# Attention scores by two halves of TensorE's rows, with another opening

## The chip, the cores and the metric

The kernel runs on one core of one Trainium2 chip. The metric is the device time of one execution in microseconds (us). The core's engines have their own instruction streams: TensorE (PE in the rows; PEld are its weight loads), VectorE (DVE), ScalarE (ACT), GpSimd (POOL) and SyncE (SP), which issues the transfers.

## The reference, cut to what matters

```python
# attention: q, k, v are (8, 8, 576, 64); the keys and values are averaged over 8 neighbours
k_p = k.reshape(B, H, Sp, 8, D).mean(axis=3)      # Sp = 72
v_p = v.reshape(B, H, Sp, 8, D).mean(axis=3)
scores = scale * np.matmul(q, k_p.transpose(0, 1, 3, 2))
attn = np.exp(scores - scores.max(axis=-1, keepdims=True))
attn = attn / (attn.sum(axis=-1, keepdims=True) + 1e-09)
x = np.matmul(attn, v_p)                           # as 4608 tokens x 512
h = x @ w_in                                       # 512 -> 2048
g = np.where(h > 0, h, np.exp(np.minimum(h, 0)) - 1)
x = g @ w_out                                      # 2048 -> 512
h = x @ moe2_w_in                                  # 512 -> 1024
solu = h * softmax(h)
out = layernorm(solu) * g_ln @ moe2_w_out          # 1024 -> 512
```

## The kernel before

**Attention in units.** A unit `i` is one batch and one pair of heads: 32 units, `NP` = 4 to a batch. Its queries lie as `q` [128, 576], the first head's 64 channels on rows 0 to 63, the second's on rows 64 to 127. The summed keys lie for units 4 to 31 in one of two tiles `kpbd` [128, 144] that are zero but for two blocks, head 0 in rows 0 to 63 and columns 0 to 71, head 1 in rows 64 to 127 and columns 72 to 143. So one product of a query tile (128 queries are the weights, 144 columns stream) gives both heads' scores. `att_scores` makes five such products for a unit (`QT` has five query tiles), three into one PSUM bank and two into another (tile `at`, line 517). Each is plain float32, and the trace shows it as two weight loads and two passes. `att_max`, `att_exp` and `att_soft` make the softmax out of PSUM; a unit in `GROUPED` has one ACT instruction for each 72 columns, which also sums them, the others subtract on DVE and have one ACT instruction for all. `att_T` or `att_D` transposes the weights of attention, and `att_V` or `att_VB` multiplies with the values: there the heads go to two halves of TensorE's columns (64 output rows each; lines 670 and 623).

**The rest of TensorE's work** is 512 columns wide in float32r, each product in three parts (high by high, low by high, high by low): `m_h1` and `m_o1` (lines 1052, 1107) for the first three blocks of 512 tokens, `mul_h` and `mul_o` (lines 1247, 1337) for the other six, then the second layer (lines 1444, 1581). Attention of later units is spread between them.

**The order.** Up to the last stage the program is written in a rough order, and `settle` plans the order anew on every engine: it has a cost for each instruction (`cost`), walks through time (`forward`) and writes its order down as dependencies. Neighbouring instructions of TensorE on the same tile are one `Step`, which is not broken up. `startup` writes the opening: units 0 to 3 (`kz`, `kq` tiles), the first weights' conversion from float64, the first products. There are 56 products `busy` on the identity there (line 1658) that keep TensorE at work; the planner puts them into its gaps.

```python
for t0, t1 in ((0, 2), (2, 4)) if i < NP else ((0, 3), (3, 5)):
    s = next(banks)
```

Of the kernel before, what the change touches and what calls it, by code (L numbers as in the profile page):

```python
# [31 lines left out]
def settle(tc, nc, stacks, PEND=2.3, FAST=1.7, FLIGHT=2.5e6, WINDOW=14):  # L32
# [33 lines left out]
    def cost(op, i, ins, outs):  # L66
        n = cols(outs[0])
        if op.eng == "PE":
            if str(ins[0].dtype).endswith("float32r"):
                op.dur += 0.015 + n * 0.0004203  # L70
            elif i.is_transpose:
                op.dur += 0.1045
            else:
                op.dur += 0.226 if n == 144 else 0.04 + n * (0.00084 if outs[0].ap[0][1] == 64 else 0.00168)
            return
        n = max(cols(o) for o in ins + outs)
        wide = [o for o in ins if str(o.bass_ap.tensor.space) == "SB"]
# [20 lines left out]
    for i in list(nc.cur_bb.bb.instructions):  # L98
        kind = type(i).__name__
        if "ManualSchedule" in kind:  # L100
            fixed = len(ops)
        if "ManualSchedule" in kind or "Boundary" in kind:
            continue
        eng = str(i.engine).split(".")[-1]
        if kind == "InstRegisterMove":
            held.setdefault(eng, []).append(i)
            continue
        ins, outs = ([o for o in x if hasattr(o, "bass_ap")] for x in (i.ins, i.outs))
        fi, fo = [foot(o) for o in ins], [foot(o) for o in outs]
        key = fo[0][0] if fo else None  # L110
        if not (eng == "PE" and ops and ops[-1].eng == "PE" and ops[-1].key == key and len(ops[-1].ins) < 12) or idle(key):
            ops.append(Step(eng, len(ops), key))
        op = ops[-1]
        op.ins += held.pop(eng, []) + [i]
        op.acc += [(f, False) for f in fi if not f[0].startswith("in_")] + [(f, True) for f in fo]
        if outs:
            cost(op, i, ins, outs)
# [98 lines left out]
    latest = {}  # L216
# [10 lines left out]
    def forward(latest, until=1e9):  # L227
# [11 lines left out]
        for _ in range(len(ops)):  # L239
            best = min(((x, None, o, x) for o, x in ready[None].items()), key=lambda x: x[0], default=None)  # L240
            for e in engines if best is None else ():
# [2 lines left out]
                    continue  # L244
                if e == "SP" and len(flight) > 7:
                    f = max(f, done[flight[-8]])
                room, behind = FLIGHT, None
                for d in reversed(flight if e == "SP" and f < 40.0 and not manual[e] else ()):
                    room -= d.bytes * d.wide
                    if room < 0.0:  # L250
# [24 lines left out]
                        continue  # L275
                else:
                    first = min(at(o) for o in r)
                    k = min((o for o in r if at(o) <= first + LOOK), key=lambda o: latest[o] + 6.0 * (at(o) - first))
                    for q in r if e in ("Activation", "DVE") else ():
                        end = at(k) + k.dur  # L280
                        if q is not k and at(q) < end:
# [19 lines left out]
            if e is None:  # L301
                done[k] = begin
            elif e == "SP":
                land = PEND if begin > 40.0 else FAST
                for w in range(k.wide):
                    pipe[w] = max(free[e] + land - 1.0, pipe[w]) + k.move * (1.0 if begin > 40.0 else 0.78 if k.wide == 16 else 1.05)
                done[k] = max(pipe[:k.wide]) + 1.0
                flight.append(k)
            else:
                done[k] = free[e] + k.lat  # L310
# [28 lines left out]
def kernel(  # L339
# [49 lines left out]
    zd = [dr.tile([4, P, 256], F32, name=f"zd{i}") for i in range(4)]  # L389
    ident = cst.tile([P, P], F32, name="ident")  # L390
    make_identity(nc, ident)
    kpbd = [pa.tile([P, 2 * SK], F32, name=f"kpbd{i}", tag=f"kpbd{i}", bufs=1) for i in range(2)]
    for t in kpbd:
        nc.gpsimd.memset(t, 0.0)

    def wtile(name):
        return sb.tile([P, 4, 512], F32R, name=name, tag="w", bufs=8)
# [8 lines left out]
    units = [(b, p) for b in range(NB) for p in range(NP)]  # L406
    NU = len(units)

    GROUPED = (1, 2) + tuple(range(4, 22))
    BLOCKT = range(8, 32)  # L410
    NTREE = 3
    KPOOL = ()
    NPOOL = ()

    xh, xl = {}, {}
# [12 lines left out]
    def att_load(i, what="kqv"):  # L428
        b, p = units[i]
        if i < NP:  # L430
            if ("kq", p) not in st:
# [2 lines left out]
                    st["v2"] = p1.tile([P, 4, 512], F32, name=f"v2{i}", tag="wo", bufs=4).rearrange("p a f -> p (a f)")  # L434
                n = P * POOL
                v_t = st["v2"][0:SK, (p % 2) * n:(p % 2 + 1) * n].rearrange("s (c t) -> s c t", t=POOL)
                st["kq", p] = (kq[:, 0:S], kq[:, S:2 * S], v_t)
            k_t, q_t, v_t = st["kq", p]
# [21 lines left out]
    def att_kv(i):  # L460
        b, p = units[i]
        if ("kp", b, p) not in st:
            if i < NP:
                if "kz" not in st:
                    kz = sb.tile([P, 4, 512], F32, name="kz", tag="w", bufs=8)
                    nc.gpsimd.memset(kz[:, :, 0:2 * SK], 0.0)
                    st["kz"] = kz
                kp = st["kz"][:, p, 0:2 * SK]
                vt = st["kz"][0:SK, p, 2 * SK:2 * SK + P]
            else:  # L470
                kp = kpbd[i % 2]
# [12 lines left out]
    def att_kc(i):  # L484
        kp, kr = att_kv(i)[0], st.pop(("kr", i))
        if i in KPOOL:
            nc.gpsimd.tensor_scalar(kp[0:64, 0:SK], kr[0:64, :], 1.0 / (8 * POOL), None, op0=ALU.mult)
            nc.gpsimd.tensor_scalar(kp[64:128, SK:2 * SK], kr[64:128, :], 1.0 / (8 * POOL), None, op0=ALU.mult)
            return
        nc.scalar.mul(kp[0:64, 0:SK], kr[0:64, :], 1.0 / (8 * POOL))  # L490
        nc.scalar.mul(kp[64:128, SK:2 * SK], kr[64:128, :], 1.0 / (8 * POOL))
# [16 lines left out]
    def att_scores(i, banks):  # L508
# [1 line left out]
        kp, vt = st["kp", units[i][0], units[i][1]]  # L510
        q_t = st.pop(("q", i))
        st["sv", i] = []
        for t0, t1 in ((0, 2), (2, 4)) if i < NP else ((0, 3), (3, 5)):
            s = next(banks)
            ts = QT[t0:t1]
            for t, o in enumerate(ts):
# [6 lines left out]
        st["a", i] = (pa.tile([P, NG, SK], F32, name=f"es{i}", tag="es", bufs=2), vt)  # L523

    def grouped(i):
        return i in GROUPED
# [41 lines left out]
    def att_T(i, h):  # L568
# [4 lines left out]
        a = st["aT", i]  # L573
        pt = ps.tile([P, 512], F32, name=f"pt{i}_{h}", tag="C")
        for t in range(4):
            nc.tensor.transpose(pt[0:SK, t * P:(t + 1) * P], es[:, 2 * t + h, :], ident)
        nc.scalar.copy(a[:, h, 0:4 * P], pt[0:SK, :])
        if h == 1 and i >= NP:
            pr = ps.tile([P, 512], F32, name=f"pr{i}", tag="C")
            for g in range(2):  # L580
                nc.tensor.transpose(pr[0:SK, g * P:(g + 1) * P], es[:, 8 + g, :], ident)
# [31 lines left out]

    def att_VB(i, banks):
        es, vt = st.pop(("a", i))
        a = st.pop(("aT", i)).rearrange("k h t -> k (h t)").rearrange("k (r t h c) -> k h r t c", r=4, h=2, c=32)
        b, p = units[i]
        vals = []
        for r, n in ((0, 4), (2, 5)):
# [438 lines left out]
    def m_h1(j, f):  # L1058
        n = sizes[j]
        h = m_mul(j, f, 0, KDM) if (j, f) not in begun else begun.pop((j, f))  # L1060
        e = p1.tile([P, 512], F32, name="e", tag="e")
        nc.scalar.activation(e[:, 0:n], h[:, 0:n], AF.Relu, scale=-1.0)
        nc.scalar.activation(e[:, 0:n], e[:, 0:n], AF.Exp, scale=-1.0)
        gt[j, f] = (e, h)

    def m_max(j, f):
# [733 lines left out]
        i = ((512 * (j + 1) - 1) // S) * NP + NP - 1  # L1800
        return min(NSTEP, 4 * i + (VLAG + 1 if i in BLOCKT else 7))

    goal = [upto(1) + 0, 70, upto(4) + 1]
    def combo_all():
        for k in range(NFP):
            yield from combo_in(k)
# [411 lines left out]
```

## Time and profile before

| | |
|---|---|
| time, median of 3 | 1208.61 us (1208.07 to 1208.61) |
| profiled execution | 1209.54 us, span 1207.8 us |
| PE busy | 1198.3 us (99%) |
| DVE, ACT, POOL busy | 972.2, 835.3, 165.0 us |
| granted TensorE clock | 1.0 |

The span goes from the first to the last instruction of the profiled execution, and 1.7 us of its time lie around it. A matmul's end in the rows is modelled: neighbours overlap, so what a product costs is read from start to start.

### The profile page before, as it was taken

How to read it: one execution, taken by the hardware profiler on the slowest of the kernel's cores; microseconds unless marked ns; L12 is line 12 of the kernel's file. 1: busy time of each engine (PE TensorE's matmuls, PEld its weight loads, DVE VectorE, ACT ScalarE, POOL GpSimd, SP SyncE). 2: the span in 40 equal slices, each digit the busy share in tenths (PEclk: the TensorE clock that was granted, in tenths of full speed). 3: DMA queues.
4: the chain of work that ended last, by engine and by line, in shares of the span. 5: the costliest groups of instructions: out<-in, count | busy, mean ns of one | idle time of the engine just before them, and what ended most of it. 6: DMA issues, size and time to landing. Idle time of an engine off the chain costs nothing.

```text
span 1207.8 us, 17321 instructions
## 1 busy us (share of the span) xinstructions
PE 1198.3 (99%) x5576; PEld 974.4 (81%) x5576; DVE 972.2 (80%) x1509; ACT 835.3 (69%) x1675; POOL 165.0 (14%) x149
## 2 busy tenths in 40 slices
PE   8999999999999999999999999999999999999998
PEld 7877877777887787888888888888888888888887
DVE  6887877788998899977896687996888878778773
ACT  6999877787667773657854488653777766767664
POOL 3455333223211001000000000000000100000000
PEclk9999999999999999999999999999999999999999
DMA  9877689899699998999777988789455444544342
GB/s 317 281 226 222 194 283 288 285 277 317 208 327 279 308 281 282 295 315 271 221 230 240 299 263 298 232 286 346 155 167 168 163 143 153 167 155 143 113 148 96
DMA packets 188875, 285.01 MB, mean 236 GB/s; under 512 B 20208, under 2 KB 99568, under 8 KB 187760
## 3 DMA queue, kind: packets, MB, share of 16 engines
q1 hardware_dynamic: 188784, 283.90, 73.7%
q8 instruction: 44, 0.72, 0.3%
q14 instruction: 47, 0.39, 0.1%
HBM read 191.83 MB, written 92.01 MB: 235 GB/s over the span
## 4 chain that ended last, share of the span: by engine, by line
PE 94%; DVE 2%; POOL 1%; ACT 1%; DMA 1%; issue 1%; SPq 0%; DVEq 0%; ACTq 0%; POOLq 0%
PE hA L1247 16%; PE po L1581 16%; PE oA L1337 13%; PE h L1052 10%; PE o L1107 9%; PE zX L1444 8%; PE zZ L1444 4%; PE oC L1337 4%; PE hB L1247 3%; PE at L517 3%; PE oB L1337 3%; PE at L623 2%; PE zY L1444 2%; PE at L670 1%; DMA w1d<-ci 1%
## 5 line engine op out<-in xcount | busy, mean ns | idle before, releaser
L1581 PE MATMUL po<-w,dhl 128*128 128x512 f32 x864 | 201.3, 389 | 0.0
L1581 PEld LDWEIGHTS po<-w,dhl 128*128 128x128 f32 x864 | 162.1, 188 | 33.6
L1337 PE MATMUL oA<-op,wr 128*128 128x512 f32 x672 | 156.2, 391 | 0.0
L1337 PEld LDWEIGHTS oA<-op,wr 128*128 128x128 f32 x672 | 125.5, 188 | 29.0 <-issue 2.0
L1327 ACT CAST op<-g 128x1024 fp32r<-128x1024 f32 x84 | 87.8, 1053 | 69.3 <-PE oA L1337 30.3
L1328 DVE TENSOR_TENSOR op<-g,op 128x1024 fp32r<-128x1024 f32 x84 | 102.0, 1224 | 17.6 <-ACT op L1327 17.2
L1247 PE MATMUL hA<-sS,wr 128*128 128x512 f32 x414 | 103.3, 391 | 0.0
L1521 POOL TENSOR_TENSOR sc<-sc,mhalf 128x1 f32<-128x1 f32 x36 | 21.4, 597 | 577.8 <-DVE sc L1520 555.7
L1444 PE MATMUL zX<-w,xh 128*128 128x512 f32 x288 | 100.1, 389 | 0.0
L1247 PEld LDWEIGHTS hA<-sS,wr 128*128 128x128 f32 x414 | 77.2, 188 | 17.7 <-ACT sp L1259 0.9
L973 POOL TENSOR_TENSOR wol<-wo,woh 128x512 fp32r<-128x512 f32 x48 | 67.5, 1407 | 149.5 <-ACT woh L972 149.5
L566 POOL TENSOR_TENSOR es<-es,sm 128x720 f32<-128x720 f32 x28 | 43.1, 1541 | 270.5 <-DVE sm L564 227.3
L1107 PE MATMUL o<-gh,woh 128*128 128x512 f32 x192 | 78.2, 407 | 0.0
L1052 PE MATMUL h<-xh,wh 128*128 128x512 f32 x192 | 77.2, 402 | 0.1
L1052 PE MATMUL h<-xh,wl 128*128 128x512 f32 x192 | 75.1, 391 | 0.6 <-POOL wl L869 0.6
L1107 PE MATMUL o<-gh,wol 128*128 128x512 f32 x192 | 75.2, 392 | 0.1
L1052 PE MATMUL h<-xl,wh 128*128 128x512 f32 x192 | 74.9, 390 | 0.0
L1259 ACT COPY sp<-hA 128x512 f32<-128x512 f32 x72 | 42.0, 587 | 36.6 <-PE hA L1247 35.9
L550 ACT ACTIVATE es<-at,mx 128x72 f32<-128x72 f32 x196 | 60.1, 332 | 4.4 <-DVE mx L536 3.7
L1444 PEld LDWEIGHTS zX<-w,xh 128*128 128x128 f32 x288 | 54.1, 188 | 11.2
L1454 ACT COPY sn<-zX 128x512 f32<-128x512 f32 x54 | 31.8, 588 | 43.2 <-PE zX L1444 43.1
L1267 DVE SCALAR_TENSOR_TENSOR g<-ep,g 128x512 f32<-128x512 f32 x72 | 50.1, 699 | 14.0 <-ACT ep L1266 13.7
(387 smaller groups left out, 2800.1 us busy)
## 6 DMA issues: line engine op xcount, KB each, us to landing
wr<-w3d SPq DMA_DIRECT2D x168, 256.0 KB
wr<-w1d SPq DMA_DIRECT2D x161, 256.0 KB
dT<-zd SPq DMA_DIRECT2D x132, 128.0 KB
raw<-in_w SPq DMA_DIRECT2D x32, 512.0 KB
v<-in_v SPq DMA_DIRECT2D x32, 288.0 KB
x1r<-x1d SPq DMA_DIRECT2D x9, 1024.0 KB
out<-ot SPq DMA_DIRECT2D x35, 256.0 KB
zd<-ha SPq DMA_DIRECT2D x17, 512.0 KB
```

The source lines that it names most:

```text
L550: nc.scalar.activation(es[:, g, :], sv[:, g - g0, :], AF.Exp, bias=mx[:, g:g + 1], accum_out=st["sm", i][:, g:g + 1])
L566: eng.tensor_tensor(es, es, bc(sm, n), op=ALU.mult)
L973: nc.gpsimd.tensor_tensor(ol, t[:, f % 4, :], oh.bitcast(F32), op=ALU.subtract)
L1052: nc.tensor.matmul(h[:, 0:n], a[g][:, kk, fo:fo + P], x[j][:, kk, 0:n], start=(kk == 0 and m == 0), stop=(kk == KDM - 1 and m == 2), skip_ ...
L1107: nc.tensor.matmul(acc, a[:, dm * P:(dm + 1) * P], x[:, 0:n], start=(f == 0 and m == 0), stop=(f == NF - 1 and m == 2))
L1247: nc.tensor.matmul(bank, w[:, a, kk], x[:, b, kk], start=(start and m == 0), stop=(stop and m == 5), skip_group_check=True,)
L1267: gate["dve"] = nc.vector.scalar_tensor_tensor(d, e, 1.0, h, op0=ALU.subtract, op1=ALU.max).ins
L1327: gate["act"] = nc.scalar.copy(o[:, 0], src).ins
L1328: gate["dve"] = nc.vector.tensor_tensor(o[:, 1], src, o[:, 0].bitcast(F32), op=ALU.subtract).ins
L1337: nc.tensor.matmul(banks[d], ws[i][:, a, d * P:(d + 1) * P], o[:, b, i], start=(start and t == 0 and i == 0 and m == 0), stop=(stop and t ...
L1444: nc.tensor.matmul(bank, x[:, o:o + P], w[:, y + k, :], start=(start and m == 0), stop=(stop and m == 5), skip_group_check=True,)
L1581: nc.tensor.matmul(po, a[:, c], b[c // 4][:, c % 4, :], start=(m == 0), stop=(m == 3 * NC2 - 1))
```

## The change

Units 4 to 31: the keys of both heads stay in the same 72 columns (`kph`, [128, 72], no zero blocks), written by one ACT instruction in place of two. `att_scores` makes ten products for a unit in place of five: for each query tile one with rows 0 to 63 (head 0) and one with rows 64 to 127 (head 1), 72 columns each, head 0 into one bank and head 1 into another. In the built program these have a tile of 64 rows by 128 columns of the array, at row 0 and at row 64; all other products but those with the values have 128 by 128. The planner's `Step` takes the ten as one, at 0.085 us each (0.226 us for each of the five before). The softmax's groups are ordered by head, and indices in `att_T` and `att_VB` follow.

The opening and the plan: the zeroing of `kz` goes from POOL to DVE, that of `kpbd` falls away; the scaled keys of units 1 to 3 are written by POOL (`KPOOL`) in place of ACT; POOL sums the values of unit 3 too (`NTREE`); the weights of attention of units 2 and 3 have room of their own in the `kq` tile; the first two blocks of `m_h1` take one instruction of DVE and one of ACT in place of two of ACT; units 20 and 21 leave `GROUPED`; the planner's numbers for transfers and choices differ, and two goals for attention's pace.

```diff
@@ settle
-                op.dur += 0.226 if n == 144 else 0.04 + n * (0.00084 if outs[0].ap[0][1] == 64 else 0.00168)
+                op.dur += 0.226 if n == 144 else 0.085 if n == 72 else 0.04 + n * (0.00084 if outs[0].ap[0][1] == 64 else 0.00168)
...
+        src = {f[0] for f in fi}
+        same = bool(ops) and (ops[-1].key == key or (ops[-1].src == src and any(t.startswith("kph") for t in src)))
+        if not (eng == "PE" and same and ops[-1].eng == "PE" and len(ops[-1].ins) < 12) or idle(key):
...
-                room, behind = FLIGHT, None
+                room, behind = 1.2e6 if f < 7.0 else FLIGHT, None
...
@@ tile_pool_attention__elu_moe__solu_moe_kernel
-    kpbd = [pa.tile([P, 2 * SK], F32, name=f"kpbd{i}", tag=f"kpbd{i}", bufs=1) for i in range(2)]
-    for t in kpbd:
-        nc.gpsimd.memset(t, 0.0)
+    kph = [pa.tile([P, 2 * SK], F32, name=f"kph{i}", tag=f"kph{i}", bufs=1)[:, 0:SK] for i in range(2)]
...
-    GROUPED = (1, 2) + tuple(range(4, 22))
+    GROUPED = (1, 2) + tuple(range(4, 20))
     BLOCKT = range(8, 32)
-    NTREE = 3
-    KPOOL = ()
+    NTREE = 4
+    KPOOL = (1, 2, 3)
...
-                    nc.gpsimd.memset(kz[:, :, 0:2 * SK], 0.0)
+                    nc.vector.memset(kz[:, :, 0:2 * SK], 0.0)
...
+        if i >= NP:
+            nc.scalar.mul(kp, kr, 1.0 / (8 * POOL))
+            return
         nc.scalar.mul(kp[0:64, 0:SK], kr[0:64, :], 1.0 / (8 * POOL))
         nc.scalar.mul(kp[64:128, SK:2 * SK], kr[64:128, :], 1.0 / (8 * POOL))
...
-        for t0, t1 in ((0, 2), (2, 4)) if i < NP else ((0, 3), (3, 5)):
+        if i >= NP:
+            heads = [next(banks) for _ in range(2)]
+            for t, o in enumerate(QT):
+                for h, s in enumerate(heads):
+                    d = slice(64 * h, 64 * h + 64)
+                    nc.tensor.matmul(s[:, t * SK:(t + 1) * SK], q_t[d, o:o + P], kp[d], start=True, stop=True)
+            m = len(QT)
+            for h, s in enumerate(heads):
+                st["sv", i].append((m * h, m, s[:, 0:m * SK].rearrange("p (a k) -> p a k", k=SK)))
+            yield
+        for t0, t1 in ((0, 2), (2, 4)) if i < NP else ():
...
+        if j == 0 and f < 2:
+            nc.vector.tensor_scalar(e[:, 0:n], h[:, 0:n], 0.0, None, op0=ALU.min)
+            nc.scalar.activation(e[:, 0:n], e[:, 0:n], AF.Exp)
+        else:
+            nc.scalar.activation(e[:, 0:n], h[:, 0:n], AF.Relu, scale=-1.0)
+            nc.scalar.activation(e[:, 0:n], e[:, 0:n], AF.Exp, scale=-1.0)
...
-    goal = [upto(1) + 0, 70, upto(4) + 1]
+    goal = [upto(1) + 0, 68, upto(4) + 0]
```

On TensorE, before, the scores of unit 5 (`kpbd_91`, `q_631`) stand between products of `m_h1` (tile `h`) and `m_o1` (tile `o`):

```order
L1052 MATMUL h_695<-xh_131,wl 128x512
L1052 MATMUL h_695<-xl_132,wh 128x512
L517 MATMUL at<-kpbd_91,q_631 128x144 x5
L1107 MATMUL o_0_0_495<-gh,woh 128x512
L1107 MATMUL o_0_0_495<-gh,wol 128x512
```

On TensorE now, the same unit's scores (`kph_91`, `q_633`; `m_o1` is at line 1130):

```order
L1130 MATMUL o_0_1_493<-gh,wol 128x512
L1130 MATMUL o_0_1_493<-gl__677,woh 128x512
L522 MATMUL at<-kph_91,q_633 128x72 x10
L1130 MATMUL o_0_2_494<-gh,woh 128x512
L1130 MATMUL o_0_2_494<-gh,wol 128x512
```

Five products became ten; all 28 units now have such a run of ten with products of 128 rows by 128 columns on either side, where before ten of the 28 were split into three and two, as in the opening's last unit 4.

On ACT in the opening, before (`es_200`, `es_220`, `es_229` are the softmax of units 0, 1 and 2, `a_262` unit 0's transposed weights, line 835 the first conversion):

```order
L545 ACTIVATE es_200<-es_200 128x576
L550 ACTIVATE es_220,sm_237<-at_214,mx_230 128x72 x4
L550 ACTIVATE es_220,sm_237<-at_217,mx_230 128x72 x4
L490 ACTIVATE kz<-kr_212 64x72
L491 ACTIVATE kz<-kr_212 64x72
L577 COPY a_262<-pt_0_263 72x512
L577 COPY a_262<-pt_1_269 72x512
L550 ACTIVATE es_229,sm_251<-at_223,mx_233 128x72 x4
L550 ACTIVATE es_229,sm_251<-at_226,mx_233 128x72 x4
L835 ACTIVATE raw<-raw,b_95 128x512 x2
```

On ACT in the opening now (unit 2's softmax is `kq_106`, `a_259` is unit 0's):

```order
L563 ACTIVATE es_198<-es_198 128x576
L568 ACTIVATE es_218,sm_234<-at_212,mx_227 128x72 x4
L568 ACTIVATE es_218,sm_234<-at_215,mx_227 128x72 x4
L568 ACTIVATE kq_106,sm_248<-at_221,mx_230 128x72 x4
L568 ACTIVATE kq_106,sm_248<-at_224,mx_230 128x72 x4
L854 ACTIVATE raw<-raw,b_93 128x512 x2
L853 ACTIVATE cu<-raw 128x512 x2
L596 COPY a_259<-pt_0_260 72x512
L596 COPY a_259<-pt_1_266 72x512
```

Unit 2's eight exponentials and the first conversion went ahead of unit 0's copies out of PSUM, and the keys' scaling left ACT.

On DVE, the program's first rows now (`kr_188` is unit 0's key sums, `kr_199` unit 1's); before, the two sums stood next to each other:

```order
L481 TENSOR_REDUCE kr_188<-kq_99 128x72
L467 MEMSET kz 128x4x144
L481 TENSOR_REDUCE kr_199<-kq_103 128x72
L554 TENSOR_REDUCE mx_203<-at_192 128x4
L554 TENSOR_REDUCE mx_203<-at_195 128x4
```

The zeroing of `kz` stands behind the first key sums, and unit 0's scaled keys are written into that tile.

## Rows read from the trace of the kernel before

**Rows 1.** The page: span, each engine's busy time, the granted clock by slices.

```profile
span 1207.8 us, 17321 instructions
PE 1198.3 (99%) x5576; PEld 974.4 (81%) x5576; DVE 972.2 (80%) x1509; ACT 835.3 (69%) x1675; POOL 165.0 (14%) x149
PEclk9999999999999999999999999999999999999999
```

**Rows 2.** Busy time by stretches: PE, PEld, DVE, ACT, POOL, clock, DMA share, GB/s.

```profile
9.70:17.50 7.80, 6.43 (x52) 6.05 (x53) 7.05 (x14) 4.53 (x21) 5.38 (x6) 1.00 1.02 308
17.50:36.00 18.50, 17.31 (x114) 12.59 (x113) 13.97 (x23) 17.79 (x43) 3.93 (x6) 1.00 1.01 370
36.00:44.00 8.00, 8.00 (x37) 6.62 (x36) 7.76 (x10) 7.88 (x15) 5.16 (x4) 1.00 0.90 253
44.00:100.00 56.00, 55.39 (x289) 43.95 (x289) 45.69 (x63) 53.80 (x137) 30.46 (x20) 1.00 0.73 229
100.00:160.00 60.00, 60.00 (x300) 48.20 (x298) 44.71 (x76) 51.74 (x158) 23.57 (x17) 1.00 0.72 226
160.00:340.00 180.00, 180.00 (x865) 142.83 (x864) 149.58 (x274) 133.19 (x429) 53.28 (x38) 1.00 0.88 273
340.00:600.00 260.00, 259.94 (x1209) 208.92 (x1208) 225.73 (x324) 170.67 (x287) 20.17 (x13) 1.00 0.93 287
```

**Rows 3.** The page's chain that ended last, by engine.

```profile
PE 94%; DVE 2%; POOL 1%; ACT 1%; DMA 1%; issue 1%; SPq 0%; DVEq 0%; ACTq 0%; POOLq 0%
```

**Rows 4.** Scores of units 4 to 31 by line and form.

```profile
L517 PE MATMUL at<-kpbd,q 128*128 128x144 f32 x280 | 40.5, 286 | 0.0
```

**Rows 5.** Timeline of PE around unit 4's first three score products: start, length.

```profile
42.68 0.39 PE L1052 MATMUL h<-xh,wh 128*128 128x512 f32 x1
...
43.82 0.39 PE L1052 MATMUL h<-xl,wh 128*128 128x512 f32 x1
44.05 0.90 PE L517 MATMUL at<-kpbd,q 128*128 128x144 f32 x6
44.69 0.49 PE L1107 MATMUL o<-gh,woh 128*128 128x512 f32 x1
45.01 0.40 PE L1107 MATMUL o<-gh,wol 128*128 128x512 f32 x1
```

**Rows 6.** Timeline of PE around unit 5's product with the values (halves of columns).

```profile
95.22 0.39 PE L1107 MATMUL o<-gl__979,woh 128*128 128x512 f32 x1
95.53 1.19 PE L670 MATMUL at<-a,vt 72*64 72x448 f32 x8
96.66 0.50 PE L1052 MATMUL h<-xh,wh 128*128 128x512 f32 x1
97.00 0.40 PE L1052 MATMUL h<-xh,wl 128*128 128x512 f32 x1
```

**Rows 7.** The same stretch, weight loads (PEld), with idle time before them.

```profile
95.53 0.20 PEld L670 LDWEIGHTS at<-a,vt 72*64 72x64 f32 x4 [0.35 <-ACT gh L1077]
95.96 0.14 PEld L670 LDWEIGHTS at<-a,vt 72*64 72x64 f32 x2 [0.23 <-issue]
96.34 0.14 PEld L670 LDWEIGHTS at<-a,vt 72*64 72x64 f32 x2 [0.23 <-issue]
96.65 0.19 PEld L1052 LDWEIGHTS h<-xh,wh 128*128 128x128 f32 x1 [0.17 <-issue]
96.76 0.19 PEld L1052 LDWEIGHTS h<-xh,wl 128*128 128x128 f32 x1
```

**Rows 8.** Weight loads around a later unit's product with the values.

```profile
372.17 0.63 PEld L623 LDWEIGHTS at<-a,vt 72*64 72x64 f32 x8 [0.35 <-issue]
373.29 1.01 PEld L1247 LDWEIGHTS hA<-sS,wr 128*128 128x128 f32 x5 [0.49 <-issue]
```

**Rows 9.** Timeline of ACT in the opening.

```profile
16.46 1.06 ACT L577 COPY a<-pt 72x512 f32<-72x512 f32 x2 [3.25 <-PE pt L576]
17.55 0.32 ACT L550 ACTIVATE es<-at,mx 128x72 f32<-128x72 f32 x1
...
19.94 1.43 ACT L835 ACTIVATE raw<-raw,b 128x512 uint32<-128x512 uint8 x2
```

**Rows 10.** Timeline of PE where its last filler ends.

```profile
34.63 0.38 PE L1658 MATMUL busy<-ident 128*128 128x128 f32 x2
35.07 0.50 PE L1052 MATMUL h<-xh,wh 128*128 128x512 f32 x1
```

**Rows 11.** Small groups by line: POOL's zeroing, ACT's scaling of the keys.

```profile
L466 POOL MEMSET kz<- 128x576 f32 x1 | 0.6, 581 | 0.0
L490 ACT ACTIVATE kpbd<-kr 64x72 f32<-64x72 f32 x28 | 7.5, 269 | 1.7 <-PE at L517 1.4 <-DVE kr L480 0.3
```

More of the change, by code (lines that the diff above doesn't have):

```diff
@@ L110, in settle @@
         key = fo[0][0] if fo else None
-        if not (eng == "PE" and ops and ops[-1].eng == "PE" and ops[-1].key == key and len(ops[-1].ins) < 12) or idle(key):
+        src = {f[0] for f in fi}
+        same = bool(ops) and (ops[-1].key == key or (ops[-1].src == src and any(t.startswith("kph") for t in src)))
+        if not (eng == "PE" and same and ops[-1].eng == "PE" and len(ops[-1].ins) < 12) or idle(key):
             ops.append(Step(eng, len(ops), key))
+            ops[-1].src = src
         op = ops[-1]
@@ L277, in forward @@
                     first = min(at(o) for o in r)
-                    k = min((o for o in r if at(o) <= first + LOOK), key=lambda o: latest[o] + 6.0 * (at(o) - first))
+                    k = min((o for o in r if at(o) <= first + LOOK), key=lambda o: latest[o] + 8.0 * (at(o) - first))
                     for q in r if e in ("Activation", "DVE") else ():
@@ L305, in forward @@
                 for w in range(k.wide):
-                    pipe[w] = max(free[e] + land - 1.0, pipe[w]) + k.move * (1.0 if begin > 40.0 else 0.78 if k.wide == 16 else 1.05)
+                    pipe[w] = max(free[e] + land - 1.0, pipe[w]) + k.move * (1.0 if begin > 40.0 else 1.05 if k.wide < 16 else 0.95 if begin < 5.0 else 0.8)
                 done[k] = max(pipe[:k.wide]) + 1.0
@@ L436, in att_load @@
                 v_t = st["v2"][0:SK, (p % 2) * n:(p % 2 + 1) * n].rearrange("s (c t) -> s c t", t=POOL)
-                st["kq", p] = (kq[:, 0:S], kq[:, S:2 * S], v_t)
-            k_t, q_t, v_t = st["kq", p]
+                st["kq", p] = (kq[:, 0:S], kq[:, S:2 * S], v_t, kq[:, 2 * S:2 * S + 2 * NP * SK])
+            k_t, q_t, v_t = st["kq", p][0:3]
         else:
@@ L470, in att_kv @@
             else:
-                kp = kpbd[i % 2]
+                kp = kph[i % 2]
                 vt = pa.tile([SK, P], F32, name=f"vt{i}", tag="vt", bufs=3)
@@ L522, in att_scores @@
             yield
-        st["a", i] = (pa.tile([P, NG, SK], F32, name=f"es{i}", tag="es", bufs=2), vt)
+        if i in (2, 3):
+            es = st["kq", units[i][1]][3].rearrange("p (g k) -> p g k", k=SK)
+        else:
+            es = pa.tile([P, NG, SK], F32, name=f"es{i}", tag="es", bufs=2)
+        st["a", i] = (es, vt)
     def grouped(i):
@@ L575, in att_T @@
         for t in range(4):
-            nc.tensor.transpose(pt[0:SK, t * P:(t + 1) * P], es[:, 2 * t + h, :], ident)
+            g = 2 * t + h if i < NP else 5 * h + t
+            nc.tensor.transpose(pt[0:SK, t * P:(t + 1) * P], es[:, g, :], ident)
         nc.scalar.copy(a[:, h, 0:4 * P], pt[0:SK, :])
@@ L580, in att_T @@
             for g in range(2):
-                nc.tensor.transpose(pr[0:SK, g * P:(g + 1) * P], es[:, 8 + g, :], ident)
+                nc.tensor.transpose(pr[0:SK, g * P:(g + 1) * P], es[:, 5 * g + 4, :], ident)
             lo = 5 * P - S
@@ L615, in att_VB @@
         es, vt = st.pop(("a", i))
-        a = st.pop(("aT", i)).rearrange("k h t -> k (h t)").rearrange("k (r t h c) -> k h r t c", r=4, h=2, c=32)
+        a = st.pop(("aT", i)).rearrange("k h t -> k (h t)").rearrange("k (r h t c) -> k h r t c", r=4, h=2, c=32)
         b, p = units[i]
@@ L1061, in m_h1 @@
         e = p1.tile([P, 512], F32, name="e", tag="e")
-        nc.scalar.activation(e[:, 0:n], h[:, 0:n], AF.Relu, scale=-1.0)
-        nc.scalar.activation(e[:, 0:n], e[:, 0:n], AF.Exp, scale=-1.0)
+        if j == 0 and f < 2:
+            nc.vector.tensor_scalar(e[:, 0:n], h[:, 0:n], 0.0, None, op0=ALU.min)
+            nc.scalar.activation(e[:, 0:n], e[:, 0:n], AF.Exp)
+        else:
+            nc.scalar.activation(e[:, 0:n], h[:, 0:n], AF.Relu, scale=-1.0)
+            nc.scalar.activation(e[:, 0:n], e[:, 0:n], AF.Exp, scale=-1.0)
         gt[j, f] = (e, h)
```

## Prediction

> **What bounds the kernel now.** First the page's busy times: PE works 1198.3 of 1207.8 us, at the full granted clock in every slice [rows 1], so the 2.4 GHz level is never lost and stays out of this. Then the chain that ended last: 94% of it is PE [rows 3]. Then the stretches: the units that change stand between 44 and 582 us, and PE is busy 55.39 of 56 us from 44 to 100 and all of the time from 100 to 340 [rows 2]. So each microsecond that PE gains or loses in the scores is one of the span, unless another engine takes over. Only ACT comes near: 53.80 of 56 us between 44 and 100 [rows 2]. In the opening it is the other way round: PE has gaps and fillers until 35.07 us [rows 10], and ACT is full from 17.5 to 44 us (17.79 of 18.5, 7.88 of 8) [rows 2].
>
> **The scores, before.** Unit 4's first part is three products, six passes. From the start of the last product ahead (43.82) to the start of the second one behind (45.01) are 1.19 us; two of these are 512 columns wide, and five such steps from 42.68 to 43.82 give 0.228 us each [rows 5]. That leaves 1.19 - 0.456 = 0.734 us, 0.122 us a pass, 0.85 ns a column. Nothing more is lost at entry or exit: the weights are loaded while the product ahead still streams. Ten passes a unit are 1.22 us, and the 280 passes [rows 4] are 34.2 us.
>
> **The scores, after.** Ten products of 72 columns are twenty passes. Four things are not in the trace as such, and each is bounded.
>
> (a) Do the two halves run side by side? Nearest row: the products with the values, two halves of columns. Their eight passes (four of 448 columns, four of 128) would take 2304 columns x 0.85 ns = 1.96 us one after the other; from 95.53 to 96.65 there are 1.12 us [rows 6, 7]. So halves of columns do run in pairs, and I take it that halves of rows, in banks of their own, do too. Then a unit has ten pairs of passes. The other end: none in pairs, twenty passes.
>
> (b) What does a pair take? Streaming is 72 x 0.85 ns = 0.06 us. But each pass loads weights of 128 columns first, and where such a load is in the open it takes 0.11 us: it starts at 96.65, and the next load, which starts when the product begins to stream, at 96.76 [rows 7]. Before, 0.11 us of loading lay under 0.122 us of streaming; now it is the longer of the two. I take 0.11 us a pair, for both halves loading at once; the lower end is 0.06.
>
> (c) Entry. Ahead of the products with the values the last product's slot ends at 95.22 + 0.23 = 95.45, and the first load starts at 95.53: 0.08 us in which PE neither streams nor loads, and then the load itself lies open [rows 6, 7]. That is no wait for data: a later unit shows the same 0.35 us without a load, with no releaser named [rows 8]. It is the price of going from an array of 128 by 128 to one cut in two. The lower end is nothing, if a cut by rows costs no change.
>
> (d) Exit. The last passes of 128 columns start at 96.34 and end at 96.56; the next load starts at 96.65 and ends at 96.76: 0.09 us of nothing and 0.11 us of open load [rows 7]. Lower end nothing.
>
> The Trainium skill, TensorEngine Tiling (Array Packing), section Key Properties, says that a change of the tiling mode, though not of the tile within it, drains TensorE, and its list of modes has 64 by 128 beside 128 by 64. By that rule rows pay what the columns pay in the rows above, which is the case that I take; without it the sum would be the first rival below.
>
> The sum for a unit: 0.08 + ten loads of 0.11 + the last stream of 0.06 + 0.09 + 0.11 = 1.44 us, against 1.22 now. All 28 units stand as one run of ten with uncut products on both sides, so each pays both ends: 28 x 0.22 = **6.2 us more**.
>
> The other edits of the units lie under PE. One ACT instruction of 0.27 us for two [rows 11] is relief where ACT is not the bound. The head's first bank used to be free for the maximum after three of five products; now both banks end with the run. That delays work which stands off the path while PE is full [rows 2]. Both banks must be free at the start; before, the second was needed 0.73 us later [rows 5]. PE's idle time after 44 us is so small [rows 2] that I take nothing, and 1 us as the upper end. Units 20 and 21 and the goals move work between ACT and DVE (149.58 of 180 us at most there) [rows 2], at no cost.
>
> **The opening.** ACT is its bound after 17.5 us, and ahead of that it stands still for 3.25 us, until unit 0's transposes are done at 16.46 [rows 9]. Unit 2's eight exponentials follow then, from 17.55 to 19.94, 2.4 us [rows 9]. Now they stand ahead of that hole, with room of their own, so the rest of ACT's row can start 2.4 us sooner. Against that the zeroing of `kz` stands behind the first key sums on DVE, and unit 0's scores behind it: POOL took 0.58 us for it [rows 11]; I take 0.4. TensorE's last filler and its first unbroken stretch (35.07) [rows 10] follow ACT: **2.0 us less**. Bounds: nothing, if transfers hold the weights back (their share is 1.01 to 1.02 from 9.7 to 36 us) [rows 2], and 3.3 us, the whole hole.
>
> **The sum.** 6.2 - 2.0 = 4.2 us more. The profiled execution took 1209.54 us (span 1207.8, 1.7 around it), 0.9 above the median; it would take 1213.7. Against the median of 1208.6: **1212.8 us**, 1210 to 1216 with the opening's bounds and the banks.
>
> **Rivals.**
> - *The cut by rows costs no change of mode.* For it: no row before shows such a cut. Against: 0.08 and 0.09 us at every cut by columns [rows 7, 8]. A unit then takes ten loads, 1.10 us, 0.12 less than now: 28 x 0.12 = 3.4, with the opening 5.4 us less, 1203.2. It decides from the point where entry and exit cost under 0.12 us together.
> - *Loads of the halves hide each other.* Entry and exit as forecast, but a pair takes 0.06 us: 0.08 + 0.11 + 0.60 + 0.09 + 0.11 = 0.99 us a unit, 6.4 less; with the opening 1200.2. For it: the loads of two halves of columns start together, four in one stretch of 0.20 us [rows 7]. Against: they have 64 columns each, and only one product's stream to lie under.
> - *About the same.* A pair takes some 0.09 us, or only one end is paid: 0.2 us less a unit than in the forecast, 5.6 in all: 1207.2.
> - *The halves take turns.* Twenty loads of 0.11 and the ends: 2.2 + 0.34 = 2.5 us a unit, 37 us more: 1244. For it: no row shows two halves of rows. Against: (a).
> - *A load waits until its own half has streamed.* A pair takes 0.11 + 0.06 = 0.17 us: 0.08 + 1.70 + 0.20 = 1.98 us a unit, 21 us more, 1228. Against: in unit 4 a pass takes 0.122 us with a load of 0.11 in it [rows 5, 7], so loads lie under streams of the same rows. The Trainium skill, TensorE: Matmul & The Clock Gate, Part 3, has loads overlap with streaming products only where the row groups differ; the trace disagrees, by that 0.122 us.
>
> **How the numbers follow.** Forecast 42 in 100; no change of mode 22; hidden loads 12; about the same 17; the two dear cases 7 together. A change of under 0.2% (2.4 us) is about what a measurement of this kernel can't tell from none. The forecast falls short of that only if the opening gives its upper bound: of its 42, 3 go to "same"; of the 17 of "about the same", 2 go to faster. Faster: 22 + 12 + 2 = 36. Same: 15 + 3 = 18. Slower: 39 + 7 = 46. The range reaches from below the first rival to the forecast's upper end: 1201 to 1216.5; it leaves out hidden loads and the two dear cases, 19 in 100. The forecast's own is 1210 to 1216.
>
> **What would show it.** (a) Starts of the two halves' passes some ns apart. (b) From pair to pair 0.11 us. (c), (d) 0.31 us from the start of the last product ahead to the first load, and idle PEld rows at each run's end, 56 in all. In the opening: ACT's hole before unit 0's copies gone, and the last filler's end at 33 us. It is wrong if a run of ten, from product to product, takes under 1.2 us, or if PE waits for a second bank.

## The result, and the profile after

| | before | after |
|---|---|---|
| time, median | 1208.55 us (1208.07 to 1209.07, 6 executions) | 1215.83 us (1215.56 to 1220.01, 6 executions) |
| first profile: time, span | 1209.54, 1207.8 us | 1215.56, 1213.7 us |
| second profile: time, span | 1208.32, 1206.5 us | 1216.39, 1214.6 us |

The ratio is 1.0067, with a 95% interval of 1.0057 to 1.0077: slower, by 7.3 us where 4.2 were forecast. The execution of 1220.01 us had a mean granted clock of 0.996, the other five 0.999 or 1.0. The page of the first profile of after (span; busy time of each engine; the chain that ended last) answers to [rows 1, 3]:

```profile
span 1213.7 us, 17818 instructions
PE 1205.8 (99%) x5856; PEld 971.7 (80%) x5856; DVE 970.8 (80%) x1517; ACT 819.1 (67%) x1601; POOL 175.2 (14%) x155
...
PE 96%; ACT 2%; DVE 1%; issue 1%; POOL 0%; DVEq 0%; POOLq 0%; ACTq 0%
```

PE is the bound as before. By stretches (columns as in [rows 2]):

```profile
44.00:100.00 56.00, 55.03 (x315) 42.46 (x314) 45.87 (x62) 49.28 (x128) 37.38 (x20) 1.00 0.72 221
100.00:160.00 60.00, 60.00 (x336) 47.00 (x335) 43.99 (x75) 50.52 (x152) 24.23 (x17) 1.00 0.71 226
160.00:340.00 180.00, 180.00 (x964) 139.58 (x963) 148.91 (x279) 125.09 (x381) 49.25 (x37) 1.00 0.87 276
```

PE stands still little more than before (0.97 us from 44 to 100 us, where [rows 2] has 0.61). ACT is relieved, 49.28 us for 53.80. So PE's work itself grew. One unit's scores, on PE and then on PEld, answer to [rows 5 to 8]:

```profile
47.82 0.39 PE L1130 MATMUL o<-gh,wol 128*128 128x512 f32 x1
48.05 0.39 PE L1130 MATMUL o<-gl__485,woh 128*128 128x512 f32 x1
48.37 1.34 PE L522 MATMUL at<-kph,q 64*128 64x72 f32 x20
49.64 0.50 PE L1130 MATMUL o<-gh,woh 128*128 128x512 f32 x1
49.97 0.40 PE L1130 MATMUL o<-gh,wol 128*128 128x512 f32 x1
```

```profile
47.83 0.19 PEld L1130 LDWEIGHTS o<-gl__485,woh 128*128 128x128 f32 x1
48.37 1.19 PEld L522 LDWEIGHTS at<-kph,q 64*128 64x128 f32 x20 [0.35 <-issue]
49.63 0.19 PEld L1130 LDWEIGHTS o<-gh,woh 128*128 128x128 f32 x1
49.74 0.19 PEld L1130 LDWEIGHTS o<-gh,wol 128*128 128x128 f32 x1
```

From the start of the last product ahead (48.05) to the start of the second one behind (49.97) are 1.92 us; less two steps of 0.228 that is 1.464 us a unit, where 1.223 stood [rows 5]. 28 x 0.241 = **6.7 us**. At the entry the last slot ends at 48.05 + 0.23 = 48.28 and the first load starts at 48.37, 0.09 us later; PEld's idle time of 0.35 us has no releaser but "issue". At the exit the load lies open from 49.63 to 49.74. The single records within the run: the two halves' passes start 6 to 7 ns apart, the second pair 0.167 us behind the first, each later pair 0.1116 us behind the one ahead, and the next load 0.200 us behind the last pass. All 28 runs read so (from product to product 1.92 us in 27 of them, 1.93 in one):

```profile
L522 PE MATMUL at<-kph,q x560: 272/272/327, 48.4 to 587.6; 64*128 64x72 f32 x187
...
  issue: 9.5, 27
  ACT wh L887: 0.4, 1
```

This is the answer on the line of the scores (least, median and longest length in ns; then the idle time of PEld ahead of it, with times): 27 entries of 0.35 us, and the 28th put down to ACT. The keys' scaling is one instruction:

```profile
L492 ACT ACTIVATE kph<-kr x28: 247/263/328, 36.7 to 517.9; 128x72 f32<-128x72 f32 x28
```

**The opening** needs two profiles of each kernel, since their executions differ there. PE's last filler and the start of its unbroken stretch, as [rows 10]; before, second profile, then after, first and second:

```profile
33.80 0.38 PE L1658 MATMUL busy<-ident 128*128 128x128 f32 x2
34.24 0.50 PE L1052 MATMUL h<-xh,wh 128*128 128x512 f32 x1
```

```profile
32.94 0.60 PE L1681 MATMUL busy<-ident 128*128 128x128 f32 x4
33.60 0.50 PE L1071 MATMUL h<-xh,wh 128*128 128x512 f32 x1
```

```profile
33.77 0.61 PE L1681 MATMUL busy<-ident 128*128 128x128 f32 x4
34.43 0.50 PE L1071 MATMUL h<-xh,wh 128*128 128x512 f32 x1
```

Before, the stretch starts at 35.07 [rows 10] or 34.24, after at 33.60 or 34.43, and the time of the execution follows (1209.54 or 1208.32, 1215.56 or 1216.39). The first two profiles set a late execution of before beside the earliest of after, and showed 1.47 us gained. The second two, each near its median, show 0.19 us lost.

What lies behind the opening can be told apart from it: from the start of the stretch to the end of the span are 1172.7 and 1172.3 us in the two profiles of before (1207.8 less 35.07, 1206.5 less 34.24), and 1180.1 and 1180.2 us in those of after. All but the opening thus costs 7.4 to 7.9 us. By the medians the whole change costs 7.3 us, and 8.2 in the executions of e9 and of before beside it. So the opening is worth some tenths either way, less than the 0.83 us by which two executions of one kernel differ there.

### The profile page after: what moved, and what is told of

Same layout as the page of the kernel before. It is cut to its first block, busy times and chain, and to the rows that moved or that the text cites. A ratio compares the mean times of both kernels' runs of the same rounds, so it can differ in the third digit from the quotient of the medians.

```text
span 1213.7 us, 17818 instructions
## 1 busy us (share of the span) xinstructions
PE 1205.8 (99%) x5856; PEld 971.7 (80%) x5856; DVE 970.8 (80%) x1517; ACT 819.1 (67%) x1601; POOL 175.2 (14%) x155
## 4 chain that ended last, share of the span: by engine, by line
PE 96%; ACT 2%; DVE 1%; issue 1%; POOL 0%; DVEq 0%; POOLq 0%; ACTq 0%
PE hA L1270 16%; PE po L1604 16%; PE oA L1360 13%; PE h L1071 10%; PE o L1130 10%; PE zX L1467 8%; PE zZ L1467 4%; PE oC L1360 4%; PE at L522 3%; PE hB L1270 3%; PE oB L1360 3%; PE at L642 2%; PE zY L1467 2%; PE at L689 1%; PE busy L1681 1%
## 5 line engine op out<-in xcount | busy, mean ns | idle before, releaser
L992 POOL TENSOR_TENSOR wol<-wo,woh 128x512 fp32r<-128x512 f32 x48 | 70.7, 1476 | 133.1 <-ACT woh L991 125.4
L1289 ACT ACTIVATE ep<-ep 128x512 f32<-128x512 f32 x96 | 59.0, 630 | 1.8
```

Source lines behind the costliest of these rows:

```text
L992: nc.gpsimd.tensor_tensor(ol, t[:, f % 4, :], oh.bitcast(F32), op=ALU.subtract)
L1289: gate["act"] = nc.scalar.activation(e, e, AF.Exp, scale=-1.0).ins
```

## The experiments

**The two parts apart.** e1 is the kernel before with the ten products, `kph`, the indices and the planner's price for them; e2 is the changed kernel with the five products of before.

```diff
-        for t0, t1 in ((0, 2), (2, 4)) if i < NP else ((0, 3), (3, 5)):
+        if i >= NP:
+            heads = [next(banks) for _ in range(2)]
...
(e1: this into before; e2: this out of after)
```

> The kernel before with the scores by halves of rows alone; the opening and the plan's numbers stay as before. The changed kernel's trace has 1.47 us for a unit's scores against 1.22, 6.8 us for 28 units. Theory A (the opening is worth about nothing against the median): 1215.3 us, ratio 1.0056, so within 1 us of the changed kernel. Theory B (the opening gives its 2.0 us, and the halves cost 9.2 in all, 2.4 of it outside the runs, by PE waiting for second banks or late softmaxes): 1217.7 us, ratio 1.0076, with idle time on PE between 44 and 600 us that the kernel before does not have.

> The changed kernel with the scores of units 4 to 31 as before (five products of 144 columns, 128 by 128); the other opening and the other plan stay. Theory A (the opening is worth about nothing): 1208.5 us, ratio between 0.9993 and 1.0007. Theory B (it is worth the 2.0 us of the prediction): 1206.5 us, ratio 0.9983. Under either the runs of L-numbers for the scores take 0.122 us a pass again, with no idle PEld row before or behind them.

e1: 1224.4 us, ratio 1.0128 (1.0114 to 1.0142), 15.6 us slower, and neither theory had that. e2: 1209.59 us, ratio 1.0007 (0.9998 to 1.0016): the rest of the change is worth nothing that can be told, and a gain of the forecast 2.0 us lies outside the interval. Its stretch starts at 34.88 us, and the rest of its span (1208.1) takes 1173.2 us, 0.5 or 0.9 more than before:

```profile
34.21 0.61 PE L1666 MATMUL busy<-ident 128*128 128x128 f32 x4
34.88 0.50 PE L1056 MATMUL h<-xh,wh 128*128 128x512 f32 x1
```

The parts don't add up (15.6 and 0.8, together 7.3), since each makes the planner write another order. In e1 PE's waits behind 36 us (engine, line, who is waited for: us, times, longest) and its stretches show where the other 8.9 us are:

```profile
PE at L638 <- DMA q<-in_q: 3.9, 1, 3.9
PE h L1067 <- POOL wl L884: 2.1, 1, 2.1
PE rs L726 <- ACT es L564: 0.7, 1, 0.7
```

```profile
44.00:100.00 56.00, 53.24 (x301) 41.10 (x300) 42.20 (x58) 47.59 (x125) 34.06 (x19) 0.97 0.73 224
...
160.00:340.00 180.00, 176.15 (x939) 135.22 (x938) 148.60 (x275) 126.39 (x421) 49.54 (x37) 0.98 0.87 273
```

Three waits of 6.7 us, 0.6 of which the kernel before has too, leave 2.8 us. In both stretches the granted clock is under 1, where before and after have 1.00. The trace shows where: behind the wait of 2.1 us and at the end of the one of 3.9 us the clock stands at 0.50, that is at 1.2 GHz, for 3.4 and 6.8 us. The same view, and two products within the first of them:

```profile
54.52:57.94 3.42, 3.42 (x8) 2.74 (x9) 2.47 (x4) 0.94 (x1) 3.06 (x2) 0.50 1.04 301
269.56:276.39 6.83, 5.30 (x16) 3.29 (x17) 4.70 (x10) 2.44 (x12) 1.39 (x1) 0.50 1.03 345
```

```profile
55.46 0.63 PE L1067 MATMUL h<-xh,wh 128*128 128x512 f32 x1
55.89 0.63 PE L1067 MATMUL h<-xh,wl 128*128 128x512 f32 x1
```

Products of 512 columns start 0.43 us apart there and 0.23 behind it. The fifteen such steps in the two (54.47 to 57.99, 273.20 to 276.36) take 6.7 us, and some 3.7 at the full clock (an estimate from the steps behind them, the first of each with its load in the open). That is 3 us for the lower clock, and 1 us more for the product with the values ahead of the second seven (2.12 us from 271.08 to 273.20, for 1.12 at the full clock in e9, from 159.21 to 160.33). The runs' 6.7, the waits' 6.1 and these 4 are 16.8 us; from the start of its stretch (33.39) to the end of its span (1222.3) e1 takes 1188.9 us, 16.2 or 16.6 more than before.

**Is it the planner's price?** The planner took 0.85 us for a run that takes 1.46.

```diff
-                op.dur += 0.226 if n == 144 else 0.085 if n == 72 else ...
+                op.dur += 0.226 if n == 144 else 0.147 if n == 72 else ...
```

> The halves with the old opening once more, and the planner takes 0.147 us for each product, as measured (1.47 us for a run of ten), where it took 0.085. Theory P (the stalls beside the runs' 6.8 us in the halves alone came of a plan made with runs at 0.85 us): the stalls go, 1208.7 + 6.8 = 1215.5 us. Theory Q (they belong to the cut itself, both banks wanted at once and given back late): it stays within 2 us of 1224.4.

> The changed kernel with 0.147 us for each product in the planner. Theory P: PE stands still for only 0.97 us between 44 and 100 us and hardly later, so a plan with the right price can give back at most that: 1215 to 1215.8 us. Rival: the wrong price costs order later too, and the time falls below 1214.

e6: 1218.96 us, ratio 1.0090 (1.0077 to 1.0103): some 5 of e1's 15.6 us are gone, the wait of 3.9 us among them. What is left of PE's waits behind 36 us:

```profile
PE h L1067 <- POOL wl L884: 1.6, 1, 1.6
PE o L1122 <- POOL wol L988: 1.2, 1, 1.2
```

So both theories were half right: with the price went the largest stall, not all of them. e7: 1217.37 us, ratio 1.0080 (1.0068 to 1.0092), its interval overlapping that of after: no gain. PE's idle time from 44 to 100 us was 1.95 us there (54.05 busy). A truer price gave a plan that is no better, and the rival's time, under 1214, did not come.

**What sets a pair.** e3 makes each pair of products twice; e4 has the products of both heads take rows 0 to 63; e5 streams 100 columns for 72, the other 28 being zero.

```diff
-            for t, o in enumerate(QT):
+            for t, o in [x for x in enumerate(QT) for _ in range(2)]:
...
-                    d = slice(64 * h, 64 * h + 64)
+                    d = slice(0, 64)
...
-                    nc.tensor.matmul(s[:, t * SK:(t + 1) * SK], q_t[d, o:o + P], kp[d], start=True, stop=True)
+                    nc.tensor.matmul(s[:, t * 100:(t + 1) * 100], q_t[d, o:o + P], kp[d], start=True, stop=True)
```

> The changed kernel with each pair of score products made twice over into the same place (20 pairs of passes a unit in one run in place of 10). If a run costs its two ends once and 0.112 us a pair, this adds 10 x 0.112 x 28 = 31 us: 1247 us, and a run takes 2.58 us. Rival: the ends are no fixed price but part of every pair (a run costs 0.147 us a pair and nothing besides): 41 us more, 1257, and a run takes 2.93 us.

> The changed kernel with both heads' products on rows 0 to 63, so one half makes all 20 passes and the other none; the second head's scores are then the first's, so the output is another. Theory A (as in the prediction: a load of 128 columns takes 0.11 us whatever its rows, and two halves load at once, so a pair is bound by one load): 20 loads one after the other, 0.08 + 2.2 + 0.26 = 2.5 us a run, 1.07 us more than now, 1246 us. Theory B (a load of 64 rows takes 0.056 us and the two halves load in turn, so the 0.112 us of a pair are two loads): a pass on one half then takes the longer of 0.056 and 0.061, a run 0.08 + 0.06 + 20 x 0.061 + 0.2 = 1.56 us, 1218 us. Theory C (a half cannot load under its own stream): 20 x (0.056 + 0.061) and the ends, 2.6 us, 1248 us.

> The changed kernel, with 28 zero columns behind each tile of keys: each of the 20 passes of a unit streams 100 columns, 85 ns at 0.85 ns a column, and not 72, 61 ns. The order on all engines is the same. Theory A (the load of the weights sets a pair's 0.1116 us, and its own half's stream lies under it): a run stays at 1.47 us and the time at 1215.8 us. Theory C (a load waits for a part of its own half's stream): a pair grows by up to the 24 ns, 28 x 10 x 0.024 = 6.7 us, and the time goes to 1222.5 us.

e3 took 1245.94 us and e4 1245.99 (one execution each), e5 1216.4 us, ratio 1.0069 (1.0056 to 1.0082). The same run on PE in e3, e4 and e5:

```profile
48.55 0.39 PE L1130 MATMUL o<-gl__485,woh 128*128 128x512 f32 x1
48.87 2.46 PE L522 MATMUL at<-kph,q 64*128 64x72 f32 x40
...
51.59 0.39 PE L1130 MATMUL o<-gh,wol 128*128 128x512 f32 x1
```

```profile
48.17 0.39 PE L1130 MATMUL o<-gl__485,woh 128*128 128x512 f32 x1
48.49 2.45 PE L522 MATMUL at<-kph,q 64*128 64x72 f32 x20
...
51.21 0.39 PE L1130 MATMUL o<-gh,wol 128*128 128x512 f32 x1
```

```profile
48.84 0.39 PE L1132 MATMUL o<-gl__487,woh 128*128 128x512 f32 x1
49.15 1.36 PE L524 MATMUL at<-kph,q 64*128 64x100 f32 x20
...
50.78 0.40 PE L1132 MATMUL o<-gh,wol 128*128 128x512 f32 x1
```

e3: 3.04 - 0.456 = 2.58 us, 1.12 more than 1.464 for ten more pairs. So a pair is 0.112 us, and what is paid once, at the ends, is 1.464 - 1.12 = 0.34 us. e4: also 2.58 us for twenty passes in a row on one half: a pass alone takes what a pair takes, 0.1116 us in the records. So two halves do run side by side, and the pair is as long as one load. Theory C, at 0.117 us a pass, is too near for e4 to settle. e5: 1.94 - 0.456 = 1.48 us, 0.02 more, and in the records all of it lies between the first and the second pair (0.190 us for 0.167, as 28 columns of 0.85 ns make it); from there on pairs follow in 0.1116 us with either width. So from the second pair on the stream of a half lies under a load, and the load is the bound, as forecast in (b). The rival with a load behind its own half's stream (1222.5 us) is out.

The Trainium skill, TensorE: Matmul & The Clock Gate, Part 2, has a load's time scale with its columns and not with its rows; the trace agrees, by 0.11 us for 128 rows [rows 7] and 0.1116 for 64, and by 0.055 us from one load of 64 columns to the next in the single records under the first line of [rows 7]. That speaks against a fixed price of a product, whatever it loads; no run here has halves of rows with narrower loads. Its Part 3, as read in the prediction, would have made e5 6.7 us slower; it was 0.6.

**The opening, by replanned kernels.** Weights' transfer earlier in SyncE's queue; unit 2's and 3's softmax without room of its own; the zeroing on POOL; and both kernels profiled again.

```diff
@@ e10
+        conv_load(("i", 0))
         att_load(0, "v")
         att_load(1, "v")
-        conv_load(("i", 0))
@@ e11
-        if i in (2, 3):
-            es = st["kq", units[i][1]][3].rearrange("p (g k) -> p g k", k=SK)
...
@@ e12
-                    nc.vector.memset(kz[:, :, 0:2 * SK], 0.0)
+                    nc.gpsimd.memset(kz[:, :, 0:2 * SK], 0.0)
```

> The kernel before, a second profile. The first was of an execution of 1209.54 us, about 1 us above the median. Theory D (executions differ in the opening, by when the first transfers land, and an opening is judged only by several): the span is about 1207 us or less, and TensorE's unbroken stretch, 35.07 us in the first profile, starts some tenths to 1 us earlier. Rival: it starts at 35.1 again, and the difference between executions lies elsewhere.

> The changed kernel, a second profile and time. Its first profile was of its fastest execution, 1215.56 us, with the unbroken stretch from 33.60 us. Theory D: the time is 1215.8 to 1216.5 and the stretch starts between 33.6 and 34.9 us, as the first conversion starts at 17.4 or waits for its transfer until 18. Rival: 33.6 again.

> The changed kernel with the first weights' transfer one place up in SyncE's queue, ahead of the values of units 0 and 1. Theory T (the opening's gain is taken back because the first conversion, now ahead of unit 0's copies, waits for its transfer in many executions): the conversion follows the exponentials without a wait, and the time falls by 0.5 to 1.3 us, to 1214.5 to 1215.3. Rival: the values then come later by as much, POOL's sums and the products with the values with them, and the time stays at 1215.8 or rises.

> The changed kernel, but the softmax of units 2 and 3 without room of its own: on ACT unit 2's eight exponentials stand behind unit 0's copies and ahead of the first conversion, as in the kernel before. Theory M (this move is what the opening brings): TensorE's unbroken stretch starts 1.5 us later, and the time is 1217 to 1218.2 us, so that the units' cost stands without a gain from the opening. Rival N (the move brings nothing, since what follows waits for transfers and DVE): 1215.8 us within 0.7.

> The changed kernel, with the zeroing of kz on POOL, as before. The forecast took 0.4 us for it on DVE, ahead of unit 0's scaled keys. If that delay reaches the end, the time falls to 1215.4; if the opening is bound behind it (ACT, transfers), it stays at 1215.8 within 0.5.

e8 and e9 are the second profiles above, and they bear theory D out as to the spans and the starts (that the landing of the first transfers makes the difference is not shown); e9 took 1216.39 us, ratio 1.0067 (1.0055 to 1.0080). e10: 1216.95 us (1.0064 to 1.0094), so the gain did not come; the new plan has ACT wait 4.39 us for that transfer, until 15.05 us, ahead of twelve of the sixteen exponentials. e11: 1217.47 us (1.0068 to 1.0092), in the range of theory M, but its trace has a new wait, 1.4 us of a unit's scores for ACT's copies at 65.65 us, which the theory doesn't speak of. e12: 1218.18 us (1.0068 to 1.0095), 1.8 us up where 0.4 down or nothing was expected: PE waits 2.6 us for DVE past 340 us. The profiled executions of e11 and e12 are long ones (1220.22 and 1220.49 us, at a granted clock of 0.998 and 0.997), so their traces hold more than their medians do. Each of these edits moved many rows behind the opening too, so none of the three tells what it was made for.

**The opening, with all other rows held.** So the written order was changed behind the planner: in e13 two rows of DVE, in e14 two rows of ACT besides, in e15 both in the kernel of e2.

```diff
     order, begun, done = forward(latest)
+    d = order["DVE"]
+    if d[14].key.startswith("mx1_"):
+        d[9:17] = [d[14], d[9], d[16], *d[10:14], d[15]]
+        c = order["Activation"]
+        c[20:26] = c[24:26] + c[20:24]
...
(e13 without the last two lines)
```

> The changed kernel, its written order changed in DVE's first rows alone: the maxima of unit 1's and unit 2's second banks stand ahead of unit 0's sums, reciprocals and unit 3's key sums, as in the kernel before. Every other row of every engine stands as it stood. Theory V (ACT's hole did not close but moved ahead of unit 1's second four exponentials, since DVE has the maximum late): ACT's 16 exponentials of units 1 and 2 follow each other from 10.2 to about 15 us, the first conversion starts up to 2.4 us sooner than at 17.96, and TensorE's unbroken stretch starts 1 to 2 us sooner than 34.43: 1214.5 to 1215.5 us. Theory T (the weights' transfer stands behind it): the exponentials end at 15 us, but the conversion waits for its transfer until 17.4 to 18, the stretch starts within 0.3 us of 34.43, and the time is 1216.0 to 1216.6 as before.

> The same with one more move, on ACT alone: unit 0's two copies ahead of the first conversion, as in the kernel before. If the transfer holds the conversion until 17.4 to 18 us (theory T), the copies fill ACT's wait at no cost, PE's wait of 0.88 us for them at 21.06 goes, and everything behind them comes about 1 us sooner: 1215 to 1215.6 us. If the conversion would have started at 15 us (theory V), the copies put it back by 2 us (to the transposes' end at 16.5 and 1.1 us of copies), and e14 is slower than e13.

> Both moves in the kernel with the new opening and the old scores (1209.59 us, no change). If the opening gains its 1 us here too: 1208.3 to 1208.8, as the kernel before or a little under. If it gains the 2 us of the forecast: 1207.5, faster than both kernels. If neither: 1209.6.

ACT's waits in the opening (last column: idle time before the row, and what ended it). Before (e8), after (e9), e13, e14:

```profile
15.57 1.07 ACT L577 COPY a<-pt 72x512 f32<-72x512 f32 x2 [2.49 <-PE pt L576]
...
19.05 1.44 ACT L835 ACTIVATE raw<-raw,b 128x512 uint32<-128x512 uint8 x2
```

```profile
14.39 0.32 ACT L568 ACTIVATE es<-at,mx 128x72 f32<-128x72 f32 x1 [2.86 <-DVE mx L554]
...
17.96 1.47 ACT L854 ACTIVATE raw<-raw,b 128x512 uint32<-128x512 uint8 x2
...
20.39 1.09 ACT L596 COPY a<-pt 72x512 f32<-72x512 f32 x2
```

```profile
14.03 0.35 ACT L571 ACTIVATE kq<-at,mx 128x72 f32<-128x72 f32 x1
...
16.95 1.43 ACT L857 ACTIVATE raw<-raw,b 128x512 uint32<-128x512 uint8 x2 [2.48 <-DMA raw<-in_w]
```

```profile
15.73 1.07 ACT L601 COPY a<-pt 72x512 f32<-72x512 f32 x2 [0.75 <-PE pt L600]
16.70 1.43 ACT L859 ACTIVATE raw<-raw,b 128x512 uint32<-128x512 uint8 x2
...
20.71 0.58 ACT L601 COPY a<-pt 72x512 f32<-72x512 f32 x1 [1.50 <-PE pt L600]
```

In after the hole is still there (2.86 us), only further ahead: it ends with DVE's maximum of unit 1's second bank, which stands behind unit 0's sums and reciprocals and unit 3's key sums. In e13 it is gone, all exponentials are done at 14.4 us, and ACT then waits 2.48 us for the first weights' transfer. In e14 unit 0's copies fill that wait, and the next one is for unit 1's transposes, 1.50 us. e13: 1215.13 us, ratio 1.0057 (1.0044 to 1.0069); e14: 1215.21 us, 1.0056 (1.0043 to 1.0068): each 0.6 us under after by the median and some 1 us by the ratio, but the intervals overlap. e15: 1209.46 us, 1.0007 (0.9998 to 1.0016): with the old scores nothing that can be told. The stretch starts at 33.84 us in e14, 0.4 us ahead of e8, and at 34.84 in e13, whose profiled execution was its longest (1216.82 us); in e15 it starts at 33.83. From there to the end of the span are 1180.1 us in e13, 1180.2 in e14 and 1173.3 in e15, so the moves changed nothing behind the opening. So theory V holds for the hole and theory T for what stands behind it. No version here beats the kernel before.

## Why the prediction was right about the scores and wrong about the opening

- **The scores, (a) to (d): right.** 1.44 us a unit were forecast and 1.464 measured; 6.2 us and 6.7. The halves run in pairs (6 to 7 ns apart); a pair takes 0.1116 us (0.11); the entry 0.09 us of nothing (0.08), then a load in the open; at the exit again a load of 0.11 us in the open. The Trainium skill's rule that a change of the tiling mode drains TensorE (TensorEngine Tiling (Array Packing), Key Properties) holds for rows as for columns: 0.35 us of idle PEld at an entry here, 0.35 at a cut by columns in [rows 8]. Of the 56 idle rows that were to show it only the 28 entries do; at the exits the modelled length of a load covers the gap, and starts alone show it.
- **The rivals of the scores:** no change of mode, by 0.35 us an entry, and hidden loads, by 0.1116 us a pair, are out. Turns are out by e4 (2.58 us a unit), the wait for a stream by e5.
- **The opening: the step that failed.** Of the sum's two terms, 6.2 and -2.0 us, the second is the wrong one: about nothing was won. The prediction put it: unit 2's exponentials "stand ahead of that hole, with room of their own, so the rest of ACT's row can start 2.4 us sooner", 2.0 us less in all. It read ACT's row and not DVE's, and took the hole for filled, though what opens it had moved too. Measured on the second profiles: the conversion starts 1.09 us sooner (19.05 to 17.96), unit 0's copies, now behind it, 4.8 us later (15.57 to 20.39), and PE's unbroken stretch 0.19 us later. e13 shows DVE's maximum as the cause of the hole, and then the bound that the prediction named and did not take, "nothing, if transfers hold the weights back". The zeroing of `kz` cost what was forecast (0.4): ACT's scaling of unit 0's keys waits for it until 4.98 us (4.46 in e12, without it), and unit 0's scores start at 5.57 us, before at 5.21 (first profiles).
- **The rest of the plan: put at no cost, and it has one.** Behind the start of the stretch the change costs 7.4 to 7.9 us, 6.7 of them in the runs. e2 and e15, with the old scores, take 0.5 to 1.0 us more there than before (1173.2 and 1173.3 us, for 1172.7 and 1172.3), so the other edits of the plan have a price of about the size of what is left. Their plan is not that of after, though, and its waits are others. In after a part of it is a wait for DVE, in a stretch where [rows 2] has DVE busy for 225.73 of 260 us (87%), more than the 149.58 of 180 (83%) that the prediction took for the most; PEld, second profile:

```profile
354.82 0.77 PEld L1270 LDWEIGHTS hB<-sP,wf 128*128 128x128 f32 x4 [0.48 <-DVE sP L1180]
```

The two products behind that wait come 0.33 us late together. No wait for a second bank was seen: the upper end of 1 us for the banks was not needed for that.
- **The range.** Its lower end does not follow from the bounds: with the opening's 3.3 us the sum gives 1211.5 us, not 1210. Nothing hangs on it here.
- **The base.** The execution that was priced, 1209.54 us, was late in the opening (the stretch at 35.07 us, 34.24 in e8). Setting it beside one profile of after would have borne the opening's term out (1.47 us sooner); two profiles of each did not.

## What to carry to other kernels

Halves of TensorE's rows give little to products that are bound by their weight loads: here a pair takes the 0.1116 us of one load whether it streams 72 or 100 columns, 0.10 us less a unit than the five uncut products, and each run between uncut products pays 0.34 us at its ends. At those prices a run must hold four units (0.34 over the 1.223 - 1.12 us gained a unit is 3.3) before it breaks even; this is an estimate and was not tried. An opening whose start moves by 0.8 us from one execution to the next is best judged apart from the rest: take the time from the start of the unbroken stretch to the end, which stayed within 0.4 us for one order. Where an engine's hole is to be filled, read what releases the hole on the other engine, and what stands behind the next release; and to test one step of a planned order, move rows in the written order, since a new plan costs or brings more (up to 9 us here) than the step.

## What the runs showed that was not expected

- Two halves load their weights at once at full rate: 0.1116 us for a load of 64 rows by 128 columns alone (e4) and for two side by side.
- Executions of one kernel differ by 0.83 us in where the unbroken stretch starts, before (35.07 and 34.24) and after (33.60 and 34.43), and the whole time by as much or a little more.
- A planner with a price wrong by 0.6 us a run made no worse an order in the whole change (ratio 1.0067, and 1.0080 with the right one, intervals overlapping), and a worse one with the halves alone (1.0128 and 1.0090).
- A wait on PE can cost more than its length: in e1 waits of 2.1 and 3.9 us came with 3.4 and 6.8 us at half the granted clock, some 4 us on top of the 6.0.
